# A fused attention and channel-mix kernel: converting float64 weights on ScalarE, and P V in three parts

## The chip, the cores and the metric

The kernel runs on one core of a Trainium2 chip. Its engines are TensorE (PE in the profile), VectorE (DVE), ScalarE (ACT), GpSimd (POOL) and SyncE (SP), which issues every DMA here. The metric is the device time of one execution in microseconds, the median of several runs.

## The reference

Rotary attention over 8 batches, 8 heads, 576 tokens and head size 64, followed by a channel mix over the 512 joined features:

```python
q_rot, k_rot = (rotate(q), rotate(k))
scores = scale * np.matmul(q_rot, k_rot.transpose(0, 1, 3, 2))
attn = softmax(scores)
x = np.matmul(attn, v)                  # then heads are joined: (8, 576, 512)
xk = mu_k * x + (1.0 - mu_k) * x_prev   # x_prev: x one token earlier
xr = mu_r * x + (1.0 - mu_r) * x_prev
k = np.maximum(xk @ w_k, 0.0)           # w_k: 512 x 1024
v = k * k @ w_v                         # w_v: 1024 x 512
r = 1.0 / (1.0 + np.exp(-(xr @ w_r)))   # w_r: 512 x 512
return (r * v).astype(np.float32)
```

The three weights arrive as float64, eight bytes a number. Everything else is float32.

## The kernel before

**The work.** There are 32 pairs of heads, four for each batch. A pair's queries and keys are loaded, rotated (rope, helper `combine` at L299 on VectorE or GpSimd) and multiplied in five steps to scores `s` (L432). For each of nine blocks of 128 scores rows, VectorE takes the negative maximum `nm` (L441), ScalarE the exponential `p` with its row sums (L444), and VectorE transposes `p` in 32 x 32 blocks in place (L447). Then TensorE forms the product of P with V, `av` (L507), out of 144 small matmuls per pair, 32 rows by 64 columns of the array each, and eight more that spread the reciprocal sums (L514). VectorE multiplies the two into the transposed features `xT` (L536 to L538).

When the four pairs of a batch are done, the channel mix of that batch follows, in two halves of 288 tokens. VectorE and others form the mixed inputs and split them into a high part (`mxh`) and a rest (`mxl`). Each product is three matmuls on 128 x 288 (high times high, rest times high, high times rest: L611 to L613): first the keys with `wk`, then the gate with `wr`, then the values with `wv`, whose input is the squared keys `kk`. VectorE multiplies value and gate to the output `rt` (L667). Per half there are four outputs, so 64 in all.

**The weights.** They are converted on the chip, in 20 blocks of 128 x 512: eight of `wk`, four of `wr`, eight of `wv`. `plan_convert` (L323) loads a block as pairs of 32-bit words (`raw`, one buffer), and takes the number apart. VectorE shifts the exponent out of the high word (`we`, L336), and ScalarE rebases it with an activation (L350). VectorE shifts the mantissa (`wm`, L340), joins three bits of the low word (L352) and the sign (L353). The join with the exponent (L344 on VectorE or L346 on GpSimd) gives the bits of a float32, which is split into a high part (`copy`, L303 or L305) and a rest (L299). A product can't start before the block that it needs is split.

**The order.** Nothing here is ordered by loops. Every step is an operation of a plan (`Plan`, L84) with a rank, a cost on each engine that may do it, the operations that it follows and the buffers that it uses. `issue` runs through the plan with a model of the engines, and at each moment gives a free engine the ready operation of least rank. The instructions are recorded in the order that results, engine by engine, and on the chip each engine keeps to it. The tables at L25 to L51 shift the ranks. A step that may run on two engines goes to the one that the model has free. So a change in the costs, the model or the tables moves instructions all over the kernel. SyncE's DMAs are ordered in the same way.

The product of P with V is two operations, 9 of 18 blocks (`CUT`) and the rest, between which TensorE takes other work:

## Time and profile before

| | |
|---|---|
| three runs | 1026.57, 1029.34, 1029.45 us; median 1029.34 |
| the profiled execution | 1027.46 us |
| its span, from first to last instruction | 1025.6 us |
| mean granted TensorE clock | 0.97 |
| busy TensorE / VectorE / ScalarE / GpSimd | 940.8 / 834.6 / 544.6 / 498.1 us |
| DMA | 100.4 MB, 98 GB/s |

Busy time is the union of an engine's instructions, and TensorE's ends are modelled. In a row of a group, the tile written stands left of the arrow and the tiles read right of it; then come the shape, the count, the busy time in all, the mean of one in ns, and the idle time of the engine just before them with what ended it. In a row of waits stand the time in all, how often, and the longest. In a timeline stand the start, the time taken, the engine, the line and the operation.

### The profile page before, as it was taken

Reading aid. Unit: us, or ns where it says so; the run is one execution under the profiler, and the core shown is the slowest. Engines: PE = TensorE matmul, PEld = TensorE weight load, DVE = VectorE, ACT = ScalarE, POOL = GpSimd, SP = SyncE. Lnnn points to the kernel's source line nnn. Section 1 sums busy time; section 2 is a strip of 40 time slices with the busy share of each in tenths; the row PEclk is TensorE's granted clock in tenths of the full one; section 3 lists DMA queues with packets and bytes.
Section 4 is the critical chain, followed back from the end, with each engine's and each line's share of the span. In section 5 each row is a group of like instructions: output and inputs, shape, how many; then the busy total and the mean of one; then the engine's idle time right before and its main releaser. Section 6 shows DMA issues by size and latency. Waiting matters only on the chain.

```text
span 1025.6 us, 34670 instructions
## 1 busy us (share of the span) xinstructions
PE 940.8 (92%) x15134; PEld 836.7 (82%) x15134; DVE 834.6 (81%) x1440; ACT 544.6 (53%) x1348; POOL 498.1 (49%) x581
## 2 busy tenths in 40 slices
PE   2667687999999999999999999999999999999998
PEld 1355466888789898889888899889988898988998
DVE  6999999889788898778887889788887979876552
ACT  2434445556365556556564666547554656655243
POOL 5644545455364655445464645436564756421121
PEclk9987668999999999999999999999999999999999
DMA  6434431323222233332322323332222223211000
GB/s 230 136 135 158 137 127 67 133 105 128 89 73 74 97 115 103 100 117 84 109 74 85 113 88 103 107 110 96 98 77 91 89 100 107 80 60 56 19 24 24
DMA packets 30455, 100.40 MB, mean 98 GB/s; under 512 B 3040, under 2 KB 11232, under 8 KB 26208
## 3 DMA queue, kind: packets, MB, share of 16 engines
q1 hardware_dynamic: 30304, 98.19, 27.6%
q8 instruction: 119, 1.95, 0.8%
q14 instruction: 32, 0.26, 0.1%
HBM read 88.74 MB, written 9.44 MB: 96 GB/s over the span
## 4 chain that ended last, share of the span: by engine, by line
PE 84%; DVE 11%; issue 3%; DMA 1%; ACT 1%; POOL 0%; SPq 0%; DVEq 0%; POOLq 0%; ACTq 0%
PE acc L611 20%; PE av L507 16%; PE acc L612 16%; PE acc L613 16%; PE s L432 14%; DVE p L447 2%; DVE nm L441 2%; PE av L514 1%; DVE wm L352 1%; DVE wm L353 1%; DMA turn<-in_cs 1%; DVE we L336 1%; DVE wm L340 1%; DVE wm L344 0%; DVE mxf L586 0%
## 5 line engine op out<-in xcount | busy, mean ns | idle before, releaser
L444 ACT ACTIVATE p<-s,nm 128x576 f32<-128x576 f32 x288 | 211.6, 739 | 101.1 <-DVE nm L441 97.4
L441 DVE TENSOR_REDUCE nm<-s 128x1 f32<-128x576 f32 x288 | 205.2, 745 | 27.1 <-PE s L432 25.3
L447 DVE STREAM_TRANSPOSE p<-p 128x576 f32<-128x576 f32 x288 | 210.3, 754 | 7.9 <-ACT p L444 7.8
L507 PE MATMUL av<-p,values 32*64 32x128 f32 (+1 forms) x9216 | 194.2, 303 | 23.1 <-DVE p L447 18.3
L507 PEld LDWEIGHTS av<-p,values 32*64 32x64 f32 x9216 | 168.6, 136 | 42.2 <-DVE p L447 21.6
L432 PE MATMUL s<-kh,qh 64*128 64x288 f32 (+1 forms) x738 | 140.6, 427 | 34.1 <-POOL qh L299 17.2
L611 PE MATMUL acc<-mxh,wk_h 128*128 128x288 f32 x512 | 163.4, 319 | 6.5 <-DVE wk_h L305 6.3
L611 PE MATMUL acc<-kkh,wv_h 128*128 128x288 f32 x512 | 157.6, 308 | 1.9 <-issue 1.0
L612 PE MATMUL acc<-mxl,wk_h 128*128 128x288 f32 x512 | 153.0, 299 | 2.1 <-POOL mxl L299 1.1
L613 PE MATMUL acc<-mxh,wk_l 128*128 128x288 f32 x512 | 152.6, 298 | 0.0
L612 PE MATMUL acc<-kkl,wv_h 128*128 128x288 f32 x512 | 151.0, 295 | 0.0
L613 PE MATMUL acc<-kkh,wv_l 128*128 128x288 f32 x512 | 150.7, 294 | 0.0
L299 POOL TENSOR_TENSOR mxl<-mxf,mxh 128x288 fp32r<-128x288 f32 x98 | 87.1, 896 | 117.9 <-ACT mxh L303 98.1
L432 PEld LDWEIGHTS s<-kh,qh 64*128 64x128 f32 (+1 forms) x738 | 79.6, 207 | 75.3 <-ACT p L444 19.6
L299 POOL TENSOR_TENSOR kkl<-hr,kkh 128x288 fp32r<-128x288 f32 x107 | 95.2, 897 | 76.2 <-ACT kkh L303 59.2
L611 PEld LDWEIGHTS acc<-mxh,wk_h 128*128 128x128 f32 x512 | 98.0, 191 | 25.4 <-issue 20.4
L611 PEld LDWEIGHTS acc<-kkh,wv_h 128*128 128x128 f32 x512 | 96.0, 188 | 13.4 <-issue 10.0
L586 DVE SCALAR_TENSOR_TENSOR mxf<-xT,mu_t,mxf 128x288 f32<-128x288 f32 x128 | 89.3, 715 | 18.5 <-ACT mxf L581 17.3
L612 PEld LDWEIGHTS acc<-mxl,wk_h 128*128 128x128 f32 x512 | 98.3, 192 | 3.0 <-POOL mxl L299 1.4
L613 PEld LDWEIGHTS acc<-mxh,wk_l 128*128 128x128 f32 x512 | 98.1, 192 | 0.2 <-DVE wk_l L299 0.2
L612 PEld LDWEIGHTS acc<-kkl,wv_h 128*128 128x128 f32 x512 | 96.3, 188 | 1.0 <-issue 0.9
L613 PEld LDWEIGHTS acc<-kkh,wv_l 128*128 128x128 f32 x512 | 96.2, 188 | 0.0
(90 smaller groups left out, 1705.4 us busy)
## 6 DMA issues: line engine op xcount, KB each, us to landing
values<-in_v SPq DMA_DIRECT2D x32, 1152.0 KB, 5.1
xq<-in_qt SPq DMA_DIRECT2D x32, 640.0 KB, 4.0
xk<-in_kt SPq DMA_DIRECT2D x32, 576.0 KB, 4.7
out_dram<-rt SPq DMA_DIRECT2D x64, 144.0 KB, 1.8
raw<-in_w_k SPq DMA_DIRECT2D x8, 512.0 KB, 3.2
raw<-in_w_v SPq DMA_DIRECT2D x8, 512.0 KB, 3.3
raw<-in_w_r SPq DMA_DIRECT2D x4, 512.0 KB, 4.3
turn<-in_cs SPq DMA_DIRECT2D x1, 640.0 KB, 7.8
```

Of the source, the lines that this page charges most:

```text
L299: (V if e == "V" else G).tensor_tensor(out=out, in0=a, in1=b, op=op)
L336: V.tensor_scalar(out=u("e"), in0=d["high"], scalar1=20, scalar2=0x7FF, op0=ALU.logical_shift_right, op1=ALU.bitwise_and)
L340: V.tensor_scalar(out=u("m"), in0=d["high"], scalar1=12, scalar2=9, op0=ALU.logical_shift_left, op1=ALU.logical_shift_right)
L432: T.matmul(w[x][:, h, 0:H], lhsT=kind(d[q][r, c * P:(c + 1) * P]), rhs=kind(d[k][r, h * H:(h + 1) * H]), start=i == 0, stop=i == len(todo) ...
L441: V.tensor_reduce(out=w["nm", x], in_=w[x][:, :, 0:H], op=ALU.max, axis=AX.XY, negate=True)
L444: A.activation(halves(d["pt"][:, place]), w[x][:, :, 0:H], AF.Exp, bias=w["nm", x], scale=1.0, accum_out=d["sums"][:, place + 1:place + 2])
L447: V.transpose(d["pt"][:, place], d["pt"][:, place])
L507: T.matmul(at(a, x, c0, 32 * (p1 - p0)), lhsT=d["vf"][g, b * P + x * D:b * P + x * D + D], rhs=d["pt"][g, p0:p1, 32 * b:32 * b + 32], star ...
L586: V.scalar_tensor_tensor(out=x["f"], in0=d["x", half][:, 1:1 + n], scalar=mu_t[:, m:m + 1], in1=x["f"], op0=ALU.mult, op1=ALU.add)
L611: T.matmul(w["a"], lhsT=w_h[:, i, sl], rhs=x["h"], start=(i == 0), stop=False)
L612: T.matmul(w["a"], lhsT=w_h[:, i, sl], rhs=x["l"], start=False, stop=False)
L613: T.matmul(w["a"], lhsT=w_l[:, i, sl], rhs=x["h"], start=False, stop=(i == count - 1))
```

## The change

A float64 is seen as four 16-bit quarters. The load now puts a block two bytes into a buffer that is one number longer (`raw`, 128 x 513 x 2 words), so that the 32-bit words of the buffer lie across the float64's own: `middle` holds the 32 bits under the topmost quarter. The topmost quarter (sign, exponent and four bits of the mantissa) is read in place as a 16-bit integer. ScalarE makes two activations of it, one with a positive and one with a negative scale, each of which keeps numbers of one sign. Their difference (VectorE or GpSimd) has sign, exponent and the upper bits of a float32. ScalarE multiplies `middle` by 2^-13 and GpSimd adds it. Then the block is split as before. So VectorE's four bit operations go; ScalarE has three activations per block where it had one; the joining step is a difference and an addition, the addition always on GpSimd. The four cuts at L336 to L353 are thus replaced by L345 and L351 of the new kernel.

The product of P with V is three operations of six blocks each instead of two of nine. The plan's model of how fast TensorE takes instructions is another one: before, each full 256 of them ended at least 3000 ns after the last; now any instruction stands at least 3730 ns of work behind the 256th before it. With this, all ranks have been searched anew (the tables at the head, a line of which is shown).

```diff
-CUT = 9
-WAIT = 0.1353
+CUTS = (0, 6, 12, 18)
+WAIT = 0.1207
...
-R = dict(k=44.27, q=66.09, v=57.3, cs=-364.48, ld=64.17, rope0=112.51, rope1=437.99, rope2=-790.69, split0=-68.32,
+R = dict(k=58.32, q=84.25, v=134.98, cs=-1171.54, ld=633.38, rope0=361.85, rope1=724.37, rope2=-1460.06,
...
         def load():
-            words = sb.tile([P, 512, 2], U32, tag="raw", name="raw", bufs=BUFS["raw"])
-            nc.sync.dma_start(words.rearrange("p n w -> p (n w)"), src)
-            d["low"], d["high"] = words[:, :, 0], words[:, :, 1]
...
+            words = sb.tile([P, 513, 2], U32, tag="raw", name="raw", bufs=BUFS["raw"])
+            quarters = words.rearrange("p n w -> p (n w)").bitcast(I16)
+            nc.sync.dma_start(quarters[:, 1:2049], src)
+            d["middle"] = words[:, 0:512, 1]
+            d["top"] = quarters.rearrange("p (n w) -> p n w", w=4)[:, 1:513, 0]
+
+        def signed(n, scale):
+            d[n] = sb.tile([P, 512], I32, tag="w" + n, name="w" + n, bufs=BUFS["w" + n])
+            A.activation(d[n], d["top"], AF.Relu, bias=below, scale=scale * 2.0 ** 19)
 
         o = dma(t - 3, P * 4096, load, [], [s_w])
-        e = op({"V": (dve2(512), 0, True)}, t, 0, exponent, [o], [s_w, s_e])
-        e = op("A", t, act(512) + 30, lambda: A.activation(d["e"], d["e"], AF.Relu, bias=below, scale=2.0 ** 23), [e], [s_e])
-        m = op({"V": (dve2(512), 0, True)}, t, 0, mantissa, [o], [s_w, s_m])
-        m = op({"V": (dve(512), 0, True)}, t, 0, lambda e: stt(out=u("m"), in0=d["low"], scalar=29, in1=u("m"), op0=ALU.logical_shift_right, op1=ALU.bitwise_or), [m], [s_w, s_m])
-        m = op({"V": (dve(512), 0, True)}, t, 0, lambda e: stt(out=u("m"), in0=d["high"], scalar=0x80000000, in1=u("m"), op0=ALU.bitwise_and, op1=ALU.bitwise_or), [m], [s_w, s_m])
-        m = op(two(512, B_LOW), t, 0, join, [m, e], [s_m, s_e])
+        e = op("A", t, act(512) + 30, lambda: signed("e", 1.0), [o], [s_w, s_e])
+        m = op("A", t, act(512) + 30, lambda: signed("m", -1.0), [o], [s_w, s_m])
+        m = op(two(512, B_LOW), t, 0, lambda e: combine(e, d["m"], d["e"], d["m"], ALU.subtract), [e, m], [s_m, s_e])
+        e = op("A", t, act(512) + 30, lambda: A.mul(d["e"], d["middle"], 2.0 ** -13), [m], [s_w, s_e])
+        m = op("G", t, pool(512), lambda: combine("G", d["m"], d["m"], d["e"], ALU.add), [m, e], [s_m, s_e])
...
-        o = op("T", t, 2 * CUT * 144, lambda: values(0, CUT), need, slots + [d["sp"], d["sv"]], ("row", 32 * CUT))
-        o = op("T", t + lead("av2", d["pi"]), 2 * (NB - CUT) * 144 + 2 * 137, rest, [o, d["R"]], slots + [d["sp"], d["sv"], d["srw"]], ("row", 32 * (NB - CUT) + 32))
+        for i in range(len(CUTS) - 1):
+            n, last = CUTS[i + 1] - CUTS[i], i == len(CUTS) - 2
+            need = need + [d["R"]] if last else need
+            o = op("T", t + (i * lead("av2", d["pi"])), 2 * n * 144 + 2 * 137 * last, lambda i=i: part(i), need, slots + [d["sp"], d["sv"]] + [d["srw"]] * last, ("row", 32 * (n + last)))
+            need = [o]
```

On VectorE, the last rows ahead of the first output product `rt` show both what a block costs there and where the first stage ends. Before, the last block of `wv` stands right ahead of it, with seven rows:

```order
L336 TENSOR_SCALAR we<-raw 128x512
L340 TENSOR_SCALAR wm<-raw 128x512
L352 SCALAR_TENSOR_TENSOR wm<-raw,wm 128x512
L353 SCALAR_TENSOR_TENSOR wm<-raw,wm 128x512
L344 TENSOR_TENSOR wm<-wm,we 128x512
L305 CAST wv_h<-wm 128x512
L299 TENSOR_TENSOR wv_l<-wm,wv_h 128x512
L536 TENSOR_TENSOR xT_1965<-av,rp 128x2x128
L537 TENSOR_TENSOR xT_1965<-av,rp 64x32
L538 TENSOR_TENSOR xT_1965<-av,rp 64x32
L441 TENSOR_REDUCE nm<-s 128x1
L667 TENSOR_TENSOR rt<-acc,rt 128x288
```

It is the 283rd instruction of VectorE's order (without the branch at its start). Now the same place reads:

```order
L538 TENSOR_TENSOR xT_1868<-av,rp 128x2x128
L539 TENSOR_TENSOR xT_1868<-av,rp 64x32
L540 TENSOR_TENSOR xT_1868<-av,rp 64x32
L308 TENSOR_TENSOR wm<-we,wm 128x512
L439 TENSOR_REDUCE nm<-s 128x1 x2
L445 STREAM_TRANSPOSE p<-p 128x576
L314 CAST wv_h<-wm 128x512
L445 STREAM_TRANSPOSE p<-p 128x576
L669 TENSOR_TENSOR rt<-acc,rt 128x288
```

The block has two rows left on VectorE, the difference and the high part, with attention's rows between them, and the output product is the 211th instruction. Ahead of it stand 51 maxima instead of 54, 51 transpositions instead of 53, and 27 rows of `xT` in both.

On TensorE, the place is the 21st pair's product of P with V in the steady part of the kernel. Before, its 144 matmuls stand as 72 and 72, with one product of the gate (`wr`) between:

```order
L507 MATMUL av<-p,values 64x128
L507 MATMUL av<-p,values 64x160
L611 MATMUL acc<-mxh,wr_h 128x288
L612 MATMUL acc<-mxl,wr_h 128x288
L613 MATMUL acc<-mxh,wr_l 128x288
L507 MATMUL av<-p,values 64x160
L507 MATMUL av<-p,values 64x128
```

Now they stand as 48, 48 and 48, and the second cut reads:

```order
L505 MATMUL av<-p,values 64x128
L505 MATMUL av<-p,values 64x160
L430 MATMUL s<-kh,qh 128x288 x2
L430 MATMUL s<-kh,ql 128x288 x2
L430 MATMUL s<-kl,qh 128x288 x2
L613 MATMUL acc<-mxh,wk_h 128x288
L614 MATMUL acc<-mxl,wk_h 128x288
L615 MATMUL acc<-mxh,wk_l 128x288
L505 MATMUL av<-p,values 64x160
L505 MATMUL av<-p,values 64x128
```

Nine wider matmuls now lie in that cut where one group of three lay in the only one. The first four pairs are left uncut in both orders; the other 28 have one cut before and two now.

More of the change, by code (lines that the diff above doesn't have):

```diff
@@ L17 @@
 U32 = mybir.dt.uint32
+I16 = mybir.dt.int16
 AF = mybir.ActivationFunctionType
@@ L143, in issue @@
         now, engine = 0.0, {}
-        array = dict(shape="full", place=0, line=0.0, warm=False, window=0, busy={})
+        array = dict(shape="full", index=0.0, lost=0.0, cursor=0, trail=[(0.0, 0.0)], warm=False, window=0, busy={})
         def product_time(start, cost, shape):
@@ L156, in product_time @@
             array["shape"] = kind
-            while count:
-                step = min(count, 256 - array["place"])
-                end += cost * step / shape[1]
-                count -= step
-                array["place"] += step
-                if array["place"] == 256:
-                    array["place"] = 0
-                    end = max(end, array["line"])
-                    array["line"] = end + 3000
+            steps = -(-count // 64)
+            trail = array["trail"]
+            for _ in range(steps):
+                array["index"] += count / steps
+                end += cost / steps
+                while array["cursor"] + 1 < len(trail) and trail[array["cursor"] + 1][0] <= array["index"] - 256:
+                    array["cursor"] += 1
+                work = end - array["lost"]
+                trail.append((array["index"], work))
+                if array["index"] > 256:
+                    (i0, w0), (i1, w1) = trail[array["cursor"]], trail[array["cursor"] + 1]
+                    past = w0 + (array["index"] - 256 - i0) / (i1 - i0) * (w1 - w0)
+                    late = max(0.0, 3730 - (work - past)) * count / steps / 256
+                    array["lost"] += late
+                    end += late
+            if steps == 0:
+                end += cost
             at = start
@@ L514, in shares, with part @@
                     T.matmul(at(a, x, 256, 160), lhsT=first_row[g], rhs=d["rw"][g, p0 + 1:p1 + 1], start=True, stop=True)
[L516 to L521 removed]
+        def part(i):
+            values(CUTS[i], CUTS[i + 1])
+            if i == len(CUTS) - 2:
+                shares()
+        for i in range(len(CUTS) - 1):
[3 more added lines that the diff above has]
+            need = [o]
         for half in range(2):
```

62 lines of the change are left out of this document (23 added, 39 removed).

## The prediction

> **What bounds the kernel now.** I began with the slices of the page. The rows give the busy tenths of TensorE and VectorE in 40 slices of 25.6 us, and the clock granted to TensorE.
> ```profile
> PE   2667687999999999999999999999999999999998
> DVE  6999999889788898778887889788887979876552
> PEclk9987668999999999999999999999999999999999
> ```
> There are two stages. TensorE is full from the eighth slice on; before that VectorE is the one at nine tenths. Where does the first stage end? VectorE's timeline has the first output product at 194 us, and the stage table cut there reads:
> ```profile
> 194.03 0.46 DVE L667 TENSOR_TENSOR rt<-acc,rt 128x288 f32<-128x288 f32 x1
> core 0: us, PE busy (x) PEld busy (x) DVE busy (x) ACT busy (x) POOL busy (x), PEclk, DMA share, GB/s
> 0.00:194.03 194.03, 130.47 (x1894) 96.69 (x1895) 176.03 (x282) 83.39 (x192) 95.33 (x105) 0.84 0.40 139
> 194.03:1025.60 831.57, 810.35 (x13242) 740.05 (x13240) 658.52 (x1158) 461.22 (x1157) 402.79 (x477) 1.00 0.26 88
> ```
> In the first stage VectorE is busy 176.0 of 194.0 us and idle 18.0; ScalarE is busy 83 and GpSimd 95. TensorE is idle 63.6 us and has a clock of 0.84. After it TensorE is idle 21 of 832 us. What TensorE waits for in the first stage:
> ```profile
> PE av L507 <- DVE p L447: 18.3, 5, 5.0
> PE s L432 <- POOL qh L299: 17.2, 1, 17.2
> PE s L432 <- ACT p L444: 10.4, 9, 1.9
> PE acc L611 <- DVE wk_h L305: 6.3, 1, 6.3
> PE s L432 <- DVE xT L538: 4.3, 4, 1.6
> ```
> Apart from the 17.2 us before the first product, that is the attention loop (maximum on VectorE, exponential on ScalarE, transposition on VectorE) and the converted weights. VectorE's groups of that stage show what fills it:
> ```profile
> L441 DVE TENSOR_REDUCE nm<-s 128x1 f32<-128x576 f32 x54 | 38.4, 741 | 4.0 <-PE s L432 3.7
> L447 DVE STREAM_TRANSPOSE p<-p 128x576 f32<-128x576 f32 x53 | 38.3, 750 | 0.0
> L352 DVE SCALAR_TENSOR_TENSOR wm<-raw,wm 128x512 uint32<-128x512 uint32 x20 | 15.0, 750 | 0.3
> L353 DVE SCALAR_TENSOR_TENSOR wm<-raw,wm 128x512 uint32<-128x512 uint32 x20 | 14.1, 704 | 0.3
> L336 DVE TENSOR_SCALAR we<-raw 128x512 uint32<-128x512 uint32 x20 | 12.6, 631 | 4.5 <-DMA raw<-in_w_r 3.3 <-DMA raw<-in_w_v 1.2
> L340 DVE TENSOR_SCALAR wm<-raw 128x512 uint32<-128x512 uint32 x20 | 11.6, 581 | 0.0
> L344 DVE TENSOR_TENSOR wm<-wm,we 128x512 uint32<-128x512 uint32 x10 | 8.0, 802 | 0.9
> ```
> So 53.3 us of VectorE's 176 (12.6 + 11.6 + 15.0 + 14.1) are the four bit operations of the conversion, all inside the stage that VectorE bounds.
>
> **Part one: the conversion.** The four groups go. Ahead of the first output product the order has 282 VectorE instructions before and 210 now. The difference is 80 bit operations gone; 12 differences on VectorE for 10 joins, +2; four fewer on the converted blocks; three maxima and two transpositions fewer; and 15 more of rope, mixing and squares. By the rows: -53.3, +2 x 0.80 = +1.6, -3 x 0.74 - 2 x 0.75 = -3.7; the -4 and +15 at the stage's mean of 176.03 / 282 = 0.62 us are -2.5 and +9.3. The list is 48.6 us shorter, 127.4 us. With the 18.0 us of idle time as before, the first product stands at **145.4 us**.
>
> That is an end and not the value, since the work goes elsewhere. ScalarE has two more instructions per block, 40 in all, which read 16-bit or 32-bit slices at 8-byte steps. No row shows such a read on ScalarE; the nearest is its instruction on packed words, and on VectorE the strided reads above weren't dearer than 0.42 us at best. GpSimd's addition is now in every block, and the differences that aren't on VectorE stand on it: 28 instead of 10 instructions.
> ```profile
> L350 ACT ACTIVATE we<-we,below 128x512 int32<-128x512 int32 x20 | 14.5, 723 | 45.0 <-DVE we L336 44.9
> L346 POOL TENSOR_TENSOR wm<-wm,we 128x512 int32<-128x512 int32 x10 | 12.7, 1268 | 27.8 <-DVE wm L353 27.8
> DMA to landing us min/median/max: 3.0/3.4/9.0
> L331 SPq DMA_DIRECT2D raw<-in_w_v x8: 327/328/333, 59.2 to 181.3; - x8
> L331 SPq DMA_DIRECT2D raw<-in_w_r x4: 328/328/391, 0.7 to 31.9; - x4
> ```
> ScalarE gets 40 x 0.72 = 29 us more in a stage in which it is idle for 111, GpSimd 18 x 1.27 = 23 us more where it is idle for 99. Neither is full, so the sums are covered. What is not covered is the **buffer of raw words**, of which there is one. The next load waits until a block's last reader is through, and that reader is now ScalarE's third instruction: landing 3.4 + two activations 1.44 + difference 0.80 (VectorE) or 1.27 (GpSimd) + multiplication 0.72 = 6.4 to 6.8 us, say 6.9 with the hand-overs. Before it was 3.4 + 0.63 + 0.58 + 0.75 + 0.70 = 6.1 us, and the turns took (181.3 - 0.7) / 19 = 9.5 us, so waits in the engines' queues are the rule. Nineteen turns without any wait are 131 us. With 0.7 us ahead of them and the 194.0 - 181.3 = 12.7 us that lay between the last load and the first product, that is 144.5 us, by chance the same as VectorE's list. With 1 us of waiting per turn it is 163.5 us, with the 3.4 us of before (9.5 - 6.1) 209 us. In ScalarE's new order two exponentials stand inside about half of the turns, where each waits for its maximum. I take 0.6 us per turn: **156 us**, 38 us earlier, because both lists are static and neither alone demands more than 145.5.
>
> Late next is TensorE. Its order ahead of the first output product holds the same 156 channel-mix matmuls and the same five pairs of P V, so the work behind it is the same. What is squeezed is VectorE between the first and the eighth output product: 128 instructions instead of 113, at 0.62 us 9 us more in a stretch that TensorE fills with about 85. I charge 4 us, with 0 and 9 as ends. Cover for the moved work is thus the idle time of ScalarE and GpSimd; were it gone, each 1 us per turn would cost 19.
>
> One thing speaks against moving work to GpSimd. A VectorE operation took four times its time beside a GpSimd operation and ended just after it:
> ```profile
> 15.18 1.93 POOL L299 TENSOR_TENSOR qh<-xq 128x640 f32<-128x640 f32 x1
> 15.64 1.75 DVE L336 TENSOR_SCALAR we<-raw 128x512 uint32<-128x512 uint32 x1
> L336 DVE TENSOR_SCALAR we<-raw x20: 378/416/1749, 4.1 to 186.5; 128x512 uint32<-128x512 uint32 x20
> ```
> The Trainium skill states this as a rule (SBUF — State Buffer, "Who interferes with whom"): VectorE and GpSimd share a port pair under an exclusive lock, which the one that issues second waits for. The rows agree with it (1.75 us against a median of 0.42).
> If each of the 18 added GpSimd operations held VectorE for its whole 1.27 us, 22.8 us would come on top of 145.4, which gives 168 us. But 80 of the operations that could be held are gone, and their mean above the median (0.63 against 0.42) was part of the 53.3.
>
> **Part two: P V in three parts.** In the second stage TensorE's own instruction supply is the wait:
> ```profile
> PE 84%; DVE 11%; issue 3%; DMA 1%; ACT 1%; POOL 0%; SPq 0%; DVEq 0%; POOLq 0%; ACTq 0%
> PE av L514 <- issue: 12.2, 11, 1.6
> PE av L507 <- issue: 3.2, 9, 1.0
> PE acc L612 <- issue: 1.0, 1, 1.0
> ```
> Sixteen microseconds (12.2 + 3.2 + 1.0) of TensorE's 21 idle ones come from nothing that the profile shows, nearly all in P V, and the chain counts 3% of 1025.6, some 31 us. One pair, from TensorE's timeline:
> ```profile
> 292.92 2.73 PE L507 MATMUL av<-p,values 32*64 32x160 f32 x144
> 295.57 0.40 PE L611 MATMUL acc<-mxh,wr_h 128*128 128x288 f32 x1
> 295.81 0.29 PE L612 MATMUL acc<-mxl,wr_h 128*128 128x288 f32 x1
> 295.94 0.30 PE L613 MATMUL acc<-mxh,wr_l 128*128 128x288 f32 x1
> 296.17 3.08 PE L507 MATMUL av<-p,values 32*64 32x160 f32 x139
> 300.77 0.50 PE L514 MATMUL av<-rw,first_row 32*64 32x160 f32 x8 [1.28 <-issue]
> 301.21 0.40 PE L611 MATMUL acc<-mxh,wr_h 128*128 128x288 f32 x1
> q8 instruction: 119, 1.95, 0.8%
> ```
> The first part starts 72 products in 2.65 us. The second has 80 and should take 2.94, but takes 5.04. The instruction queue's 119 packets with 1.95 MB, 16.4 KB each, show that instructions are fetched while the kernel runs. The short products of P V use them up fastest, which the wide ones between the parts, 0.13 us each, give time to refill. The new order cuts 28 of 32 pairs at 48 and 96 of 144, and from the eighth pair on has 0.4 to 4 us of other products in a cut, in place of 0.4 us in a single cut. Each further cut costs two changes of shape: 295.57 to 295.81 is 0.24 and 295.94 to 296.17 is 0.23 where 0.13 is usual, so 0.21, times 28, is 5.9 us. Against it stand stalls between 16.4 and 31 us; I take 24, of which 22 go, since half of the pairs have only 1.3 us in their two cuts. Net **-16 us**, with +6 (nothing refilled) and -25 (31 - 6) as ends.
>
> The Trainium skill calls the cost of crossing such a block of 256 instructions mostly hidden (Runtime: NRT & Kernel Launch, "Instruction fetch mechanics"). Here the trace differs, 16.4 us idle. By the page the cuts would gain nothing; that is the second rival.
>
> **Sum.** The profiled execution took 1027.5 us by its own time, 1.9 above its span and 1.9 below the median of the three runs, 1029.3. 1027.5 - 38 + 4 - 16 = 977.5; against the median, **979 us**.
>
> **Rivals.** *Conversion slower, product helped*: the raw buffer's turns or the shared port bind at 2 us of waiting per turn, first product at 182 instead of 156; 979 + 26 = 1005. For it: the turns already took 9.5 us. Against: they waited then for an engine that was 91% busy. Chance 0.12.
> *Cuts worth nothing*: the stalls stay, and the changes of shape cost 6; 979 + 22 = 1001. For it: in half of the pairs one of the two cuts still has only three products. Chance 0.13.
> *Slower than before*: the load now lands 2 bytes into its buffer, and ScalarE reads slices at 8-byte steps. If either makes a turn 10.5 us or more without waits (landing of 7 us, or activations of 1.9 us), 19 turns plus 13.4 reach 213 us, 19 later than before, and that eats the 16 us of the cuts and the rest; at 12 us a turn it is 241 us and 979 + 85 = 1064. No row shows either form; strided reads on VectorE were no dearer. Chance 0.05.
> *No relief*: ScalarE's exponentials wait behind activations that wait for words, and the stage stays at 190 us while the cuts give 6; 1029 - 4 - 6 + 4 = 1023, or just as well 1029. Chance 0.04, half of it within 0.3%.
> The forecast itself has 0.66: first product between 146 and 166 and -8 to -25 from the cuts, 960 to 995. To keep 8 in 10 the range runs from 958 (145.4 us, all stalls gone) to 1004, which takes in the second rival and the near side of the first. A change within 0.3%, about 3 us, can't be told from none. Faster 0.93, same 0.02, slower 0.05.
>
> **What would show it.** Right: VectorE's first output product near 156 us with ScalarE and GpSimd at 110 to 120 us of work ahead of it; activations of 0.7 us on the raw slices; TensorE full from the sixth or seventh slice; under 8 us of TensorE idle from issue behind it. Wrong: raw loads more than 8 us apart with ScalarE waiting for them; VectorE's differences and rope at over 1.5 us in the mean; the last part of P V still at over 4 us; or VectorE full between 156 and 240 us while TensorE waits for it.

## The result, and the profile after

The changed kernel takes 1002.16 us, the median of four runs (1000.38 to 1002.60), against 1027.95 us of the kernel before in the same session (four runs, 1025.65 to 1029.45). The ratio is 0.9748 with a 95% interval of 0.9722 to 0.9773: 25.8 us less. 979 us had been forecast, with 958 to 1004 as range: about half of the forecast gain, 2 us inside the range's upper end. The profiled execution took 1000.38 us, with a span of 998.6.

The slices of the page show the same two stages. Each is 25.0 us now.

```profile
PE   2577879999999999999999999999999999999998
DVE  5979788799868979789878979789878979775652
PEclk9967779999999999999999999999999999999999
```

TensorE is full from the seventh slice on, one earlier than before. In the first stage VectorE no longer shows a row of nines, and no other engine has taken that place. Where does the stage end now? VectorE's timeline has the first output product:

```profile
175.54 0.46 DVE L669 TENSOR_TENSOR rt<-acc,rt 128x288 f32<-128x288 f32 x1 [1.57 <-PE acc L615]
```

The stage table is cut there and at the eighth output product, at 261.76 us. Its columns are the length of the stretch, the busy times with the counts, the clock and the DMA.

```profile
core 0: us, PE busy (x) PEld busy (x) DVE busy (x) ACT busy (x) POOL busy (x), PEclk, DMA share, GB/s
0.00:175.54 175.54, 122.81 (x1882) 89.84 (x1883) 141.36 (x210) 108.20 (x226) 106.60 (x112) 0.83 0.43 151
175.54:998.60 823.06, 818.34 (x13254) 742.68 (x13252) 661.93 (x1171) 475.47 (x1186) 373.11 (x445) 1.00 0.26 90
175.54:261.76 86.22, 85.75 (x1363) 72.45 (x1362) 74.44 (x129) 43.56 (x113) 45.88 (x51) 1.00 0.33 113
261.76:998.60 736.84, 732.60 (x11894) 670.22 (x11890) 587.49 (x1044) 431.90 (x1075) 327.23 (x394) 1.00 0.26 87
```

The kernel before had its first output product at 194.03 us, the eighth at 273.99 us, and its end at 1025.64 us, so the stretches were 194.03, 79.96 and 751.65 us. The first got 18.5 us shorter (38 had been forecast), the second 6.3 longer (4), the third 14.8 shorter (16 for the cuts). In the first stage VectorE is busy 141.4 us instead of the 127.4 of the prediction and idle 34.2 instead of 18.0. Both halves of its sum were missed, 14 us by work and 16 by waits. What VectorE, GpSimd and the queue of the raw loads waited for in that stage (time in all, times, longest):

```profile
DVE wm L308 <- ACT wm L345: 10.8, 9, 4.7
DVE wv_h L314 <- POOL wm L308: 5.4, 2, 3.2
DVE xT L538 <- ACT rp L533: 3.3, 3, 1.7
```
```profile
POOL wm L308 <- ACT we L351: 16.3, 9, 3.7
POOL wm L308 <- ACT wm L345: 7.5, 6, 2.4
```
```profile
SPq L339 <- ACT we L351: 79.2, 19, 7.3
```

The first row of each comes from the new chain. The difference (`wm`, VectorE or GpSimd) waits for ScalarE's second activation, the addition on GpSimd for its third, and each of the 19 later raw loads for that third one. The tile of raw words shows the turns of its buffer:

```profile
L345 ACT ACTIVATE we<-raw,below x20: 736/762/787, 4.1 to 168.0; 128x512 int32<-128x512 int16 x20
L345 ACT ACTIVATE wm<-raw,below x20: 732/750/799, 4.7 to 168.7; 128x512 int32<-128x512 int16 x20
L351 ACT ACTIVATE we<-raw x20: 641/671/695, 6.8 to 170.3; 128x512 int32<-128x512 uint32 x20
...
L339 SPq DMA_DIRECT2D raw<-in_w_v x8: 327/328/336, 49.3 to 164.3; - x8
L339 SPq DMA_DIRECT2D raw<-in_w_r x4: 327/332/387, 0.7 to 25.4; - x4
...
DMA to landing us min/median/max: 2.9/3.4/6.1
```

The activations take 0.67 to 0.76 us and the landing 3.4 us, as priced. But 19 turns take (164.3 - 0.7) / 19 = 8.6 us each, so they hold 1.7 us of waiting over the 6.9 of work, where 0.6 had been assumed. ScalarE sat idle for 6.2 us until raw words landed. That makes 1.1 x 19 = 21 us, and the last load stands 11.2 us ahead of the first product instead of 12.7: 156 + 21 - 1.5 = 175.5.

One more wait has grown in this stage. TensorE's waits for nothing that the profile shows were 3.7 us ahead of the first output product in the kernel before; now they are 12.3:

```profile
PE av L505 <- issue: 11.0, 5, 5.9
PE av L512 <- issue: 1.3, 1, 1.3
```

The longest stands ahead of the first pair's product of P with V. The prediction looked for such waits behind the first output product alone.

Behind the first output product, one row is left of what TensorE waits for, where three with 16.4 us stood before:

```profile
PE av L512 <- issue: 0.3, 1, 0.3
```

And the product of P with V of the ninth pair, whose cuts hold the same products as those of the 21st, whose order was shown, from TensorE's timeline:

```profile
273.90 1.91 PE L505 MATMUL av<-p,values 32*64 32x160 f32 x96
...
277.52 1.91 PE L505 MATMUL av<-p,values 32*64 32x160 f32 x96
...
280.75 1.88 PE L505 MATMUL av<-p,values 32*64 32x160 f32 x95
...
282.39 0.55 PE L512 MATMUL av<-rw,first_row 32*64 32x160 f32 x15
```

The timeline shows each of a part's 48 matmuls twice, hence 96. No part has an issue wait, and between the parts lie 1.7 and 1.3 us. TensorE's share of the chain of waits has risen from 84 to 89%, VectorE's fallen from 11 to 4:

```profile
PE 89%; DVE 4%; ACT 2%; issue 2%; POOL 1%; DMA 1%; SPq 0%; DVEq 0%; POOLq 0%; ACTq 0%
```

### The profile page after: what moved, and what is told of

Its sections match the earlier page's. It is cut to its first block, busy times and chain, and to the rows that moved or that the text cites. A ratio compares the mean times of both kernels' runs of the same rounds, so it can differ in the third digit from the quotient of the medians.

```text
span 998.6 us, 34612 instructions
## 1 busy us (share of the span) xinstructions
PE 941.1 (94%) x15134; PEld 832.5 (83%) x15134; DVE 803.3 (80%) x1381; ACT 583.7 (58%) x1411; POOL 479.7 (48%) x557
## 4 chain that ended last, share of the span: by engine, by line
PE 89%; DVE 4%; ACT 2%; issue 2%; POOL 1%; DMA 1%; SPq 0%; DVEq 0%; POOLq 0%; ACTq 0%
PE acc L613 20%; PE av L505 18%; PE acc L615 17%; PE acc L614 17%; PE s L430 15%; PE av L512 1%; DVE nm L439 1%; ACT p L442 1%; DVE p L445 1%; DMA xk<-in_kt 1%; POOL wm L308 0%; DVE xT L538 0%; DVE mxf L588 0%; ACT we L345 0%; ACT rt L660 0%
## 5 line engine op out<-in xcount | busy, mean ns | idle before, releaser
L445 DVE STREAM_TRANSPOSE p<-p 128x576 f32<-128x576 f32 x288 | 213.6, 762 | 19.4 <-ACT p L442 19.2
L505 PE MATMUL av<-p,values 32*64 32x128 f32 (+1 forms) x9216 | 193.1, 301 | 14.8 <-issue 11.0
L505 PEld LDWEIGHTS av<-p,values 32*64 32x64 f32 x9216 | 164.1, 134 | 33.7 <-issue 25.6
L613 PE MATMUL acc<-kkh,wv_h 128*128 128x288 f32 x512 | 159.8, 312 | 0.1
L308 POOL TENSOR_TENSOR mxl<-mxf,mxh 128x288 fp32r<-128x288 f32 x91 | 83.0, 919 | 108.3 <-DVE mxh L314 65.1
L308 POOL TENSOR_TENSOR kkl<-hr,kkh 128x288 fp32r<-128x288 f32 x98 | 93.1, 959 | 63.9 <-ACT kkh L312 61.8
L613 PEld LDWEIGHTS acc<-kkh,wv_h 128*128 128x128 f32 x512 | 96.1, 188 | 14.5 <-issue 12.3
L588 DVE SCALAR_TENSOR_TENSOR mxf<-xT,mu_t,mxf 128x288 f32<-128x288 f32 x128 | 79.9, 640 | 5.0 <-ACT mxf L583 4.7
```

The lines of the kernel that those rows point to most:

```text
L308: (V if e == "V" else G).tensor_tensor(out=out, in0=a, in1=b, op=op)
L445: V.transpose(d["pt"][:, place], d["pt"][:, place])
L505: T.matmul(at(a, x, c0, 32 * (p1 - p0)), lhsT=d["vf"][g, b * P + x * D:b * P + x * D + D], rhs=d["pt"][g, p0:p1, 32 * b:32 * b + 32], star ...
L588: V.scalar_tensor_tensor(out=x["f"], in0=d["x", half][:, 1:1 + n], scalar=mu_t[:, m:m + 1], in1=x["f"], op0=ALU.mult, op1=ALU.add)
L613: T.matmul(w["a"], lhsT=w_h[:, i, sl], rhs=x["h"], start=(i == 0), stop=False)
```

## The experiments

Two questions were open: why the first stage gave half of what was forecast, and whether the cuts are what shortened the last stretch. The kernels ran on other chips, beside runs of the kernel before, which took 1031.9 to 1032.1 us there (three sessions, medians of 7, 7 and 13). That is 0.4% more than in the first session, so differences of 3 or 4 us between kernels of different sessions prove little by themselves, and the four runs of the changed kernel alone lie 2.2 us apart; the places of the output products are compared with 175.54 and 261.76 of the changed kernel. Where an experiment leaves out or repeats data, it says so.

For the first stage there were these theories. T1: the raw buffer's turns alone hold it. T2: the product of P with V of the first four pairs does, which TensorE takes uncut, at a mean clock of 0.62 to 1.00, in 9 to 13 us each. T3: GpSimd's longer list does, with its addition at the end of each block, by holding VectorE. T4: lists of nearly the same length wait for each other, and no single one holds it. T5: each edit adds what it gives alone (in two of the expectations it stands for something else, which is said there). And for the prediction's step itself there was S: other lists stand so close behind VectorE's, in its shade, that only part of what is taken off it arrives.

**One half raw load.** Half of each load is left out and each number read twice; there is still one buffer.

```diff
-            nc.sync.dma_start(quarters[:, 1:2049], src)
+            nc.sync.dma_start(quarters[:, 1:1025], src[:, 0:1024])
-            d["middle"] = words[:, 0:512, 1]
+            d["middle"] = words[:, 0:256, 1].unsqueeze(1).to_broadcast([P, 2, 256])
```

> The changed kernel with half of every raw load left out (256 of 512 numbers per row, each read twice by ScalarE, so half of the weights are wrong); one buffer, same order on every engine. It is the control for the run with two such buffers, and it shortens a turn of the raw buffer by what half a load takes less. First output product now at 175.5 us. Theory T1 (the turns of the one raw buffer set the first stage): with a landing of 2.6 instead of 3.4 us, 19 turns give 10 to 15 us, first product at 160 to 166. Theory T2 (the loop of attention sets it: the uncut P V of the first four pairs, 8.8 to 12.7 us each, holds TensorE and two of the three score buffers, so VectorE and ScalarE run dry there): 173 to 177. Theory T3 (VectorE is held by GpSimd's longer list through the shared path: it was busy 141.4 us, where the unhindered list was 127.4): 173 to 177.

Measured: 998.92 us (one run), first product at 172.50 us, 3.0 earlier. The landing fell to 2.6 us, as had been assumed, and T1's 10 to 15 us didn't come.

**Two half raw buffers.** The same, with two buffers in the room of one, so that a load needn't wait for the block before.

```diff
-            words = sb.tile([P, 513, 2], U32, tag="raw", name="raw", bufs=BUFS["raw"])
+            words = sb.tile([P, 257, 2], U32, tag="raw", name="raw", bufs=2)
```

> As the run with one half-size raw buffer, but with two, so that a load no longer waits for the last reader of the block before it (half of the numbers are left out and read twice). Same order on every engine. T1 (turns of the raw buffer): the first output product at 155 to 165 us instead of 175.5, and the time at 982 to 992 us. T2 (attention's loop with the uncut P V): 172 to 177, the time within 4 us of 1002. T3 (VectorE held by GpSimd): 172 to 177, within 4 us of 1002.

Measured: 999.19 us, ratio to the kernel before 0.9675 (0.9648 to 0.9703), first product at 173.21 us. The queue's wait for the third activation falls to 45.8 us, and the stage ends only 2.3 us earlier. T1 falls: the turns were slow since everything was, and with loads that come early the blocks wait elsewhere. (Two whole buffers, which would leave nothing out, were not run.)

**Half of P V in the first four pairs.** Ten of 18 blocks are computed there.

```diff
-            for b in range(b0, b1):
+            for b in (b for b in range(b0, b1) if d["pi"] >= 4 or b % 2 == 0 or b == NB - 1):
```

> The changed kernel with 8 of the 18 blocks of P V left out in the first four pairs (their outputs are wrong), same order otherwise. These four products took 10.4, 9.8, 12.7 and 8.8 us; with 10 of 18 blocks they should take about 4.5 us less each. T2 (attention's loop with the uncut P V): first output product 14 to 20 us earlier, 156 to 162, and the time down by nearly as much, 984 to 990. T1 (turns of the raw buffer): 172 to 176. T3 (VectorE held by GpSimd): 172 to 176.

Measured: 1003.17 us (one run), first product at 175.79 us. The four products take 2.7 to 5.0 us less each, 15.7 in all, and the end doesn't move. What came off them came back as a wait, which had been 1.5 us:

```profile
PE s L430 <- DVE xT L540: 15.3, 4, 4.5
```

T2 alone falls, with a reserve. The granted clock of the stage was 0.79 in this run, against 0.83 in the changed kernel's, so that TensorE's busy time fell by only 4.5 us (118.30). What the edit gives alone at the same clock was not measured.

**Small addition.** GpSimd adds 64 of 512 columns; the rest is left as the difference has it.

```diff
-combine("G", d["m"], d["m"], d["e"], ALU.add)
+combine("G", d["m"][:, 0:64], d["m"][:, 0:64], d["e"][:, 0:64], ALU.add)
```

> The changed kernel with GpSimd's addition on 64 of the 512 columns (the lower bits of the other columns are left out), same order. GpSimd's 20 additions fall from 1.35 to about 0.3 us, 20 us less on GpSimd in the first stage. T3 (VectorE held by GpSimd): VectorE's busy time ahead of the first product falls from 141 to 130 to 135 us and the first product to 162 to 168; the time to 988 to 995. T1 (turns of the raw buffer): the multiplication that ends a turn stands ahead of the addition, so 173 to 176. T2 (attention's loop): 173 to 176, the time within 3 us of 1002.

Measured: 1000.24 us, ratio 0.9687 (0.9663 to 0.9710), first product at 174.65 us. GpSimd's work falls from 106.6 to 85.2 us and VectorE's beside it from 141.4 to 136.8, and the stage gains 0.9, less than the runs of one kernel differ by. T3 alone falls.

**All three together**: two half raw buffers, half of P V in the first four pairs, and the small addition, with what each leaves out.

```diff
-            words = sb.tile([P, 513, 2], U32, tag="raw", name="raw", bufs=BUFS["raw"])
+            words = sb.tile([P, 257, 2], U32, tag="raw", name="raw", bufs=2)
-combine("G", d["m"], d["m"], d["e"], ALU.add)
+combine("G", d["m"][:, 0:64], d["m"][:, 0:64], d["e"][:, 0:64], ALU.add)
-            for b in range(b0, b1):
+            for b in (b for b in range(b0, b1) if d["pi"] >= 4 or b % 2 == 0 or b == NB - 1):
```

> The changed kernel with three reliefs at once, which alone gave 0 to 2.3 us at the first output product: two half-size raw buffers, 10 of 18 blocks of P V in the first four pairs, and GpSimd's addition on 64 columns (half of the weights' numbers, part of P V and the low bits are left out); same order. T4 (interlocked lists of nearly the same length): clearly more than the sum of the three, 3 us: first output product 8 to 20 us earlier than 175.5. T5 (something that none of the three touches, as attention's chain of score, maximum, exponential and transposition): 170 to 176.

Measured: 987.24 us (one run), first product at 162.44 us, 13.1 earlier. The three alone gave 2.3, -0.2 and 0.9, together 3.0. That is what T4 had said: while two lists stay long, the third has little to give. With all three eased, 13 us appear. It is not the only reading: the clock was 0.83 again, and if half of P V by itself gave some 10 us at this clock, the three would simply add up. The wait for `xT` shown above, which is 8.1 us here, speaks for T4.

**Small conversion.** All five converting operations work on 64 of 512 columns, except for the first block.

```diff
-            d["top"] = quarters.rearrange("p (n w) -> p n w", w=4)[:, 1:513, 0]
+            d["top"] = quarters.rearrange("p (n w) -> p n w", w=4)[:, 1:c + 1, 0]
```

> The changed kernel with the five converting operations (two activations, difference, multiplication, addition) on 64 of the 512 columns in every block but the first; loads, copies and rests are whole, the order is the same, the weights are wrong. Some 33 us less for ScalarE and 30 us less for GpSimd and VectorE together in the first stage. Theory T4 (no single list sets the first stage; the lists of all engines are interlocked and of nearly the same length, so it only gets shorter when all conversion work gets cheaper): first output product at 150 to 165 us instead of 175.5. Theory T5 (attention's own loop and the first batch's channel mix set it, and conversion lies in its shade): 171 to 176.

Measured: 993.16 us (one run). The stage table to its first output product, 8.3 us earlier:

```profile
0.00:167.23 167.23, 118.70 (x1882) 87.25 (x1883) 128.58 (x210) 85.41 (x227) 79.73 (x112) 0.87 0.46 159
```

That is between the ranges of the two theories (150 to 165 and 171 to 176) and in neither. ScalarE's 57 small activations take 0.26 to 0.35 us each. ScalarE loses 22.8 us of work, GpSimd 26.9 and VectorE 12.8, and the stage still needs 167 us. VectorE's own differences account for 3.3 of its 12.8. The rest is other operations that got cheaper when GpSimd's conversion beside them did, as in the run with the small addition, where nothing but GpSimd's work was changed and VectorE's fell by 4.6. Three of VectorE's groups of the changed kernel, and the same three here:

```profile
L588 DVE SCALAR_TENSOR_TENSOR mxf<-xT,mu_t,mxf 128x288 f32<-128x288 f32 x11 | 9.2, 860 | 1.4 <-ACT mxf L583 1.3
L308 DVE TENSOR_TENSOR xq<-xq,turn 128x640 f32<-128x640 f32 x6 | 8.8, 1484 | 0.7 <-DMA xq<-in_qt 0.7
...
L308 DVE TENSOR_TENSOR qh<-xq 128x640 f32<-128x640 f32 x4 | 5.6, 1405 | 0.0
```
```profile
L308 DVE TENSOR_TENSOR xq<-xq,turn 128x640 f32<-128x640 f32 x6 | 6.7, 1114 | 2.4 <-DMA xq<-in_qt 2.3
L588 DVE SCALAR_TENSOR_TENSOR mxf<-xT,mu_t,mxf 128x288 f32<-128x288 f32 x11 | 6.3, 591 | 0.1
...
L308 DVE TENSOR_TENSOR qh<-xq 128x640 f32<-128x640 f32 x4 | 4.2, 1047 | 0.0
```

The counts are the same and the means fall from 860 to 591, 1484 to 1114 and 1405 to 1047 ns. In the kernel before the first two stood at 664 and 1179.

**Small conversion and half of P V.** Both of those edits, with what each leaves out.

```diff
-            d["top"] = quarters.rearrange("p (n w) -> p n w", w=4)[:, 1:513, 0]
+            d["top"] = quarters.rearrange("p (n w) -> p n w", w=4)[:, 1:c + 1, 0]
-            for b in range(b0, b1):
+            for b in (b for b in range(b0, b1) if d["pi"] >= 4 or b % 2 == 0 or b == NB - 1):
```

> The changed kernel with the five converting operations on 64 of 512 columns (all but the first block) and 10 of 18 blocks of the product with V in the first four pairs; both leave out part of the computation. The first edit alone brought the first output product from 175.5 to 167.2, the second alone to 175.8. T4 (lists of nearly the same length that wait for each other): together more than the sum, first product at 152 to 163. T5 (each edit adds by itself): 165 to 168.

Measured: 982.01 us (one run), first product at 156.15 us, 19.4 earlier. Alone they gave 8.3 and -0.2, at clocks of 0.87 and 0.79; here it is 0.87, and TensorE's busy time falls by 9.9 us against the run before (118.70 to 108.80) where it had fallen by 4.5. The first product is within T4's 152 to 163 and far from T5's 165 to 168, with the same reserve: half of P V is in both sets that gave more than their sum, and its run alone had the low clock.

**The kernel before with small bit operations.** Its four bit operations work on 64 of 512 columns, which takes work off VectorE's list and adds none anywhere. The conversion's numbers are lost.

```diff
-        u = lambda n: d[n].bitcast(U32)
+        u = lambda n: d[n].bitcast(U32)[:, 0:d["cols"]]
-            d["low"], d["high"] = words[:, :, 0], words[:, :, 1]
+            d["low"], d["high"] = words[:, 0:d["cols"], 0], words[:, 0:d["cols"], 1]
```

> The kernel before with the four bit operations on VectorE on 64 of the 512 columns in every block but the first (the exponent's activation gives zero, so the weights are wrong), same order otherwise: VectorE's list loses 40 to 45 us with nothing put on ScalarE or GpSimd. The prediction's step (VectorE's list sets the first stage, what leaves it comes off the end): first output product at 149 to 155 us instead of 194. Theory S (shade: attention's loop gives a floor, the bit operations partly filled VectorE's waits in it): 165 to 180, with VectorE idle for 30 us or more in place of 18.

Measured: 1019.51 us (one run). The stage table to its first output product, and the longest of VectorE's waits in it:

```profile
0.00:181.89 181.89, 126.20 (x1894) 93.88 (x1895) 149.82 (x282) 82.78 (x192) 92.30 (x105) 0.88 0.43 149
```
```profile
DVE xT L536 <- ACT rp L531: 9.2, 5, 2.5
DVE nm L441 <- PE s L432: 6.5, 9, 1.9
```

VectorE works 26.2 us less (176.0 to 149.8) and the first product comes 12.1 us earlier, 0.46 us for each. The other 14 reappear as idle time, 32.1 us where 18.0 had been: VectorE waits for the shares of P V that ScalarE copies (`rp`) and for scores from TensorE, for which it had waited 1.5 and 3.7 us. In the kernel before these lists stood close behind VectorE's. So S holds in its mechanism; 181.9 us is 2 beyond its 165 to 180, and the list lost 26 us where 40 to 45 had been expected. This is the step on which the prediction rested, tried by itself in the kernel before, without one operation added to ScalarE or GpSimd; 149 to 155 us was clearly missed. The one run had a clock of 0.88 in this stage, against 0.84 before, so that the 12.1 us may be too many for the list alone.

**The old conversion in the new kernel.** The conversion of before, with the new tables and three parts, planned anew.

```diff
-        e = op("A", t, act(512) + 30, lambda: signed("e", 1.0), [o], [s_w, s_e])
+        e = op({"V": (dve2(512), 0, True)}, t, 0, exponent, [o], [s_w, s_e])
...
-        m = op("G", t, pool(512), lambda: combine("G", d["m"], d["m"], d["e"], ALU.add), [m, e], [s_m, s_e])
+        m = op(two(512, B_LOW), t, 0, join, [m, e], [s_m, s_e])
```

> The changed kernel with the conversion of before (six operations a block, bit operations on VectorE, a 4 KB load on the even address) and three parts kept, its order planned for that. VectorE's list ahead of the first output product gets longer by about 47 us by the rows' means. The prediction's step (VectorE's list comes off one for one): the first product at about 220 us instead of 175.5, about 1047 us in all. The rate of about 0.4 to 0.5 us for each us of that list, as the run with four small bit operations had it: the first product at 194 to 200, 1020 to 1027 us in all. Rival Z (the conversion is worth nothing, the other tables brought the first product forward): first product within 4 us of 175.5.

Measured: 1024.85 us, ratio 0.9933 (0.9907 to 0.9959). The stage table to its first and from its eighth output product:

```profile
0.00:197.92 197.92, 128.49 (x1882) 92.34 (x1882) 176.11 (x285) 83.19 (x186) 91.41 (x99) 0.82 0.38 134
286.10:1022.50 736.40, 730.34 (x11894) 668.37 (x11890) 588.03 (x1044) 431.60 (x1075) 327.24 (x394) 1.00 0.26 87
```

The first product is 22.4 us later than in the changed kernel, within the 194 to 200 of the rate of one half. One for one would have been 220 by the 47 us that were expected and 210 by the 34.7 that VectorE's work really grew by, and Z falls. (ScalarE's work falls by 25.0 and GpSimd's by 15.2 us with it, so this rate is not of VectorE's list alone.) The last stretch is the changed kernel's, 736.4 against 736.8 us. So the two parts of the change can be told apart: all of the first stage's gain is the conversion's, and none of the last stretch's.

For the last stretch there were two theories. F: the cuts save time in which TensorE waits for its instructions behind a long run of small matmuls. O: the new order around the parts made the gain, and their number doesn't matter.

**Uncut.** The first of the three operations issues all 144 matmuls of a pair in one run; the rest of the order stays.

```diff
-            values(CUTS[i], CUTS[i + 1])
+            values(0, NB if i == 0 else 0) if i == 0 else None
```

> The changed kernel with all 144 matmuls of P V put out in the first of the three parts, nothing in the second, the reciprocal sums in the third; every engine's order is otherwise the same and nothing is left out. Theory F (TensorE runs out of fetched instructions within P V, and the wider matmuls in the cuts let them be refilled): behind the first output product the stalls come back and are larger than with one cut, 1 to 2 us in each of 28 pairs, less 0.2 us for each missing change of shape, so the second stage is 20 to 40 us longer than the 823 us it takes now, and the time 1020 to 1040. Theory O (the second stage is shorter because the new tables order it better, not because of the cuts): within 5 us of 823, or some 6 us shorter.

Measured: 1054.81 us, ratio 1.0243 (1.0199 to 1.0287). What TensorE waits for behind the first output product, with a pair from its timeline:

```profile
PE av L505 <- issue: 22.0, 28, 1.2
PE s L430 <- DVE xT L540: 8.8, 5, 1.8
PE acc L614 <- DVE mxl L308: 6.1, 5, 1.2
```
```profile
278.14 3.74 PE L505 MATMUL av<-p,values 32*64 32x160 f32 x194
...
282.57 1.88 PE L505 MATMUL av<-p,values 32*64 32x128 f32 x94 [0.69 <-issue]
```

There are 28 such waits, one in each of the 24 pairs behind the eighth output product among them. There the first comes after 3.2 to 4.7 us of small matmuls in one run. The stage is 50.7 us longer (873.8 against 823.1). 22 of it are issue waits; the parts that finish later than planned make waits for VectorE beside them. The cuts do save time, more than expected.

**Two parts in the new kernel.** Two parts of nine blocks, the new conversion, planned anew.

```diff
-CUTS = (0, 6, 12, 18)
+CUTS = (0, 9, 18)
```

> The changed kernel with the product with V in two parts of 72 matmuls again, its conversion as it is, its order planned for two parts. Theory F (the cuts save the time in which TensorE waits for its instructions behind such a part, 0.4 to 2 us for each of 28 pairs): from the eighth output product to the end it takes 10 to 20 us more than the 736.8 of the changed kernel, and the whole kernel 1012 to 1020 us. Rival O (the gain after the eighth product came from the new order around the parts): within 5 us of the changed kernel. Uncut (144 in one run) had cost 52 us of span, so F also says that idle rows of TensorE put down to issue come back, some 10 to 20 us of them.

Measured: 1014.23 us, ratio 0.9816 (0.9788 to 0.9844), first product at 180.59 us. Its last stretch, and what TensorE waits for in it:

```profile
268.06:1012.90 744.84, 730.15 (x11894) 672.00 (x11892) 601.29 (x1070) 424.54 (x1053) 320.84 (x384) 1.00 0.26 86
```
```profile
PE av L512 <- issue: 4.3, 6, 0.9
PE av L505 <- issue: 3.6, 5, 0.9
```

That is 8.0 us longer than with three parts, a little under the 10 to 20 expected, and outside what O allows. But it is also 6.8 us shorter than the 751.65 of the kernel before, which cuts at the same place. (That stretch varies: with small bit operations and the same order behind them it took 755.34, and P V in it 162.8 us instead of 158.9.) Why is it shorter?

**Three parts in the kernel before.** Its own tables and its conversion, but three parts.

```diff
-        o = op("T", t, 2 * CUT * 144, lambda: values(0, CUT), need, slots + [d["sp"], d["sv"]], ("row", 32 * CUT))
+        for i in range(len(CUTS) - 1):
```

> The kernel before with its tables, its conversion and its loads, but the product with V cut in three parts for most pairs and the same planner. F (cuts save TensorE's wait for instructions): the stretch behind its first output product falls from 831.6 to 812 to 820 us and the whole to 1012 to 1018 us, if the kernel before takes 1028 beside it; the first product stays at 192 to 196. O (the new order made the gain): within 5 us of the kernel before.

Measured: 1036.17 us, ratio 1.0042 (1.0024 to 1.0061): slightly slower. F missed clearly, and the 4.3 us are within what O gave. The last stretch, and a pair from TensorE's timeline:

```profile
273.83:1034.30 760.47, 744.61 (x11916) 674.65 (x11914) 590.63 (x1043) 419.05 (x1054) 369.70 (x438) 1.00 0.25 84
```
```profile
292.86 1.91 PE L507 MATMUL av<-p,values 32*64 32x160 f32 x96
294.70 0.41 PE L615 MATMUL acc<-mxh,wr_h 128*128 128x288 f32 x1
294.94 0.29 PE L616 MATMUL acc<-mxl,wr_h 128*128 128x288 f32 x1
295.08 0.29 PE L617 MATMUL acc<-mxh,wr_l 128*128 128x288 f32 x1
295.30 1.58 PE L507 MATMUL av<-p,values 32*64 32x160 f32 x72
297.11 0.77 PE L507 MATMUL av<-p,values 32*64 32x128 f32 x24 [0.23 <-issue]
...
300.83 0.51 PE L514 MATMUL av<-rw,first_row 32*64 32x160 f32 x11 [0.32 <-issue]
```

Here, in 20 of the 24 pairs, both cuts hold only one product, three large matmuls, 0.5 us from a part's end to the next one's start; in the other four one cut is empty. The stalls come back in the second and third part. In the changed kernel the first cut is 0.9 us or more in every pair; the second is 0.5 us in half of them, and among these are six that still lose 0.3 to 0.7 us each, as no others do but the last pair. The sums over TensorE's timeline behind the eighth output product, each row counted from its start to the start of the next, show where the time goes (us; they end at TensorE's last row, so they are some 3 short of the stretch):

| kernel | parts | us between parts | P V | large products | scores | stretch |
|---|---|---|---|---|---|---|
| before | 2 | 0.5 | 158.9 | 474.9 | 114.0 | 751.7 |
| before, three parts | 3 | mostly 0.5 | 158.1 | 480.6 | 118.0 | 760.5 |
| new, two parts | 2 | 0.9 to 3.3 | 147.8 | 478.1 | 115.4 | 744.8 |
| new | 3 | 0.9 to 3.3, then 0.5 to 4.1 | 142.5 | 477.4 | 113.2 | 736.8 |

Longer cuts alone take 11.1 us off P V (158.9 to 147.8), a third part on top of them another 5.3. A third part with short cuts takes 0.8 off P V, less than that varies, and costs 9.7 in the other products, among them the changes of shape. So the cuts of the new order are worth more than those of the old one. O, that the order made the gain, is half right: the new order with two parts has 6.8 of the 14.8 us. That the length of the cuts does this is argued from the sums, and pair by pair it is not the whole cause. In the new kernel with two parts, the seven pairs with 12 or 24 large products or scores in the cut lose nothing behind it, but all five with nine lose 1.0 to 1.4 us, and of the twelve with six, half lose 0.9 to 1.4 us and half about 0.1 or less. In the kernel before with three parts, seven pairs with three products in each cut lose nothing. The place in the order matters too, and the new order with three short cuts was not run.

## Why the prediction was right and where it was wrong

**The bound of the first stage: right, and too simple.** VectorE's list was the longest, and the stage got shorter when it did. But its 18 us of idle time did not mean that only 18 us of waiting stood behind it. Two runs change that list. The one in the kernel before gives 12.1 us for 26.2 of busy time; the one in the new gives 22.4 for 34.7 (176.1 against 141.4), with other engines' work changed too.

**The step that failed** is the 0.6 us of waiting per turn of the raw buffer, and with it the sentence that 156 us would be reached "because both lists are static and neither alone demands more than 145.5". Static lists that wait for each other need more than the longest of them. The turns had 1.7 us of waiting each, and the first product stood at 175.5. One of the prediction's own signs of being wrong came true: raw loads more than 8 us apart (8.6) with ScalarE waiting for them (6.2 us). The rival *conversion slower, product helped*, with 2 us per turn, 182 us and 1005 us in all, was nearer than the forecast's own case, 960 to 995, and the result is inside the range, by 2 us, because the rivals had been taken in; that it lies inside is luck as much as foresight. The rival's mechanism, that the turns bind, was wrong too: with two buffers in place of one, 2.3 us came. That several lists hold the stage together is shown as far as the runs go by the edits that give 13.1 and 19.4 us together and 3.0 and 8.1 one by one, and by the 15.3 us of waits for `xT` in which the halved P V ended; how much of the difference is the low clock of that one run stays open. Which waits make up the remaining 156 us was not followed further; the prediction counted the same products of TensorE there as before, and did not see that its issue waits among them would grow from 3.7 to 12.3 us.

**VectorE's work ahead of the first product: 127.4 forecast, 141.4 measured.** Two terms were mis-sized. The 15 added operations were priced at the stage's mean of 0.62 us, though five of them were rope operations (`qh`, `kh`, `xq`), which take 1.4 to 1.5; that is 5 x 0.8 = 4 us of the 14. And the kept operations got dearer: the eleven mixing operations 860 instead of 664 ns, the `xq` 1484 instead of 1179. When the conversion beside them was made small, they fell back below what they had been. The prediction had seen the mechanism in one pair of rows and set it aside, because "80 of the operations that could be held are gone". They were gone, and others were held. The Trainium skill's rule (SBUF — State Buffer, "Who interferes with whom") fits what was measured: the means of VectorE's operations go with GpSimd's work beside them. But the price is not one hold for each added operation: that sum meant 127.4 + 22.8 = 150 us of VectorE's work, and 141.4 was measured. And most of what an eased GpSimd gave VectorE was lost in waits; the small addition took 4.6 us off VectorE and 0.9 off the stage.

**ScalarE and GpSimd as cover: right.** 110 to 120 us of work had been named; 108.2 and 106.6 were measured, of 175.5. The strided slices cost 0.67 to 0.76 us where 0.72 was taken, and the load at two bytes' offset landed in 3.4 us as before. The rival *slower than before* needed 1.9 us or 7 us for these and falls.

**The squeeze: right.** 4 us between 0 and 9 were charged; 86.22 - 79.96 = 6.3 came.

**P V: right in size, half right in cause.** -16 was forecast, -14.8 measured, and the rival *cuts worth nothing* falls with the uncut run. Stalls of 24 us had been assumed, of which 22 go. In the 24 pairs behind the eighth product (of the 28), what P V takes beyond an undisturbed pair's time (2.73 and 3.00 us for the two parts, 1.91, 1.91 and 2.18 for the three) adds up to 24.9 us before and 3.6 after. So 21 went. What failed is the credit: the prediction gave it to the number of parts and feared the short cuts, and the second half of that was the better half, in the sums though not in every pair. Three parts with short cuts gain nothing; two with longer ones already gain 6.8. The price of a cut was low as well. From undisturbed pairs, two parts step 2.66 + 2.93 us and three 1.84 + 1.84 + 2.11, which is 0.20 more, and the changes of shape around the extra cut add about 0.2 (275.74 to 275.98 and 277.30 to 277.52 in the changed kernel's timeline, 0.24 and 0.22 where 0.13 is usual): 0.4 and not 0.21.

The Trainium skill's word that the crossing of such a block is mostly hidden (Runtime: NRT & Kernel Launch, "Instruction fetch mechanics") does not hold for the dense run of small matmuls, if its waits are for instructions, as is argued here: uncut, TensorE waited 28 times, 22 us in all, and the kernel was 2.4% slower than before. Behind the first product of the changed kernel, where larger products stand between, the trace agrees with it: 0.3 us of idle time is left.

## What to carry to other kernels

When engines work through static lists that wait for each other, don't take the longest list's saving one for one: look how close the next lists stand, and expect about half where they are near. Easing one list alone then shows little, and edits on two or three together tell more of what holds the stage, if the clock is the same in the runs compared. For cuts in a run of small matmuls, the number of parts says little by itself: look at the work that stands in each cut and at the stall of each pair.

## What the runs showed of the hardware

- ScalarE reads 16-bit or 32-bit integers at 8-byte steps as fast as packed words: 0.75 to 0.76 and 0.67 us for 128 x 512, against 0.72.
- A load that lands two bytes off its buffer's start took 3.4 us in the median, the same as an even one.
- With P V uncut, TensorE took 3.2 to 4.7 us of small matmuls in one run, in each of the 24 pairs behind the eighth output product, before it first waited with nothing to wait for that the profile shows. That these waits are for instructions is argued from the rows (they stand nearly all in dense runs, and mostly go when large products stand between), not seen in any row.
- Between two pairs in the same kernel with the same cuts, stalls differ. In the new kernel with two parts, pairs with 0.9 us between their parts lost about 0.1 us or less when they stood in one place of the repeating order, and 0.9 to 1.4 us in another. What decides that stays open.
